# Loads of u and of unit 2's k and r moved ahead of weight strips, the flag computed inside the chain of powers, and a new order list

## The chip, the cores and the metric

The kernel runs on one core of one Trainium2 chip. The metric is the device time of one execution in microseconds (us). Before the change four runs took 508.73, 508.48, 507.45 and 509.68 us; their median is 508.6 us. Lower is better.

## What is computed

Two stages, all in float32 (the weights arrive as 64-bit words and are converted on the chip). First a linear attention with decay, for 4 batches and 8 heads of width 48 over 768 time steps, and then a feed-forward block without a non-linearity on its output:

```
cur     = einsum('bhd,bhe->bhde', u[None] * kt, vt)
y[t]    = einsum('bhd,bhde->bhe', rt, state + cur)
state   = w[None,:,:,None] * state + einsum('bhd,bhe->bhde', kt, vt)
...
x = y.transpose(0, 2, 1, 3).reshape(3072, 384)
out = (((x @ w1) * (x @ w2)) @ w3) @ w_out      # 384 -> 1024 -> 1024 -> 384
```

## The kernel before

**Units and chunks.** Time is cut into 6 chunks of 128 steps; a chunk of one batch is a unit, so there are 24 units, numbered chunk * 4 + batch. A unit's k and r (192 KB each) land in one of three `krin` buffers, its v in one of three `vnat` buffers. The decay is handled with powers of w: k and r of a unit are multiplied by the table `pn_in` (`scale`, L410) into `krs`, after which the attention inside a chunk is plain matrix products.

**Weights.** w1 and w2 come as eight strips of 768 KB (strip 0 is the first part of w1, strip 1 the first part of w2, and so on), followed by w_out and w3 in smaller pieces. They go through three `raws` buffers (`fetch`, L225) and are converted in five steps: `magnitude` on ScalarE (L360), `sign` and `high` on VectorE (L365, L368), `low` on ScalarE (L372), `total` on VectorE (L375).

**The opening** (L237 to L293) is written out by hand: the first loads on SyncE's queue; 14 dummy matmuls (`keep_busy`, L256; each shows as two in the profile); a chain of small VectorE operations (L266 to L285) that forms the powers of w in `both`; a flag that tells whether all of w lies in the range that the fast way can handle (L271, a one-row matmul L273, L287, L288); four plus four transposes of the powers (L292) and two copies into `pn_in` (L293). Every engine then reads the flag and branches (L295, L957) into one of two versions of the program. With the given data it is the fast one, and only that one runs.

**The list.** Behind the branch the order of the work on TensorE, VectorE, ScalarE and SyncE's queue is the string `ORDER` at the top of the file. Each word names a step and its indices; the kernel issues the steps in exactly that order, so each engine's order is the list with the other engines' words left out. Engines run in order; they wait for each other only where data or a buffer require it. The words that matter here (n is the unit, i the strip):

| word | step, engine | word | step, engine |
|---|---|---|---|
| kr.n, v.n, W.i | loads of k and r, of v, of a strip; SyncE's queue | U.n | `adds` (L523), TensorE: state increments, needs `krs` and `vnat` |
| d.n, e.n, f.n | `rk` (k times r, L419), `rku` (times u, L422), `dots` (sum, L426); VectorE | T.n, R.n | transposes of k and of r (L457), TensorE |
| k.n | `scale` (L410), VectorE | t.n, r.n | their copies out of PSUM (L464, L467), ScalarE |
| N.i, H.i, Q.i | `sign`, `high`, `total`; VectorE | A.n | `products` (L530), TensorE |
| M.i, L.i | `magnitude`, `low`; ScalarE | m.n | `mask` (L558), VectorE |
| g.n or h.n | `place`: the diagonal, eight ScalarE operations (L437) or one on VectorE (L431) | S.n, V.n | the unit's output in PSUM (L630, L644), TensorE |
| i.n, j.n | `state` (L541, L546, L547), VectorE | Y.n | `take`, its copy to `xT` (L652), ScalarE |
| o.n, p.n | `spread` (L555), ScalarE | a, b, c, u | x @ w1 and x @ w2 (L670), the copy (L676) and their product (L681) |
| s, B | sums for the seven-product scheme of the last matrix product (L714, L717, L701), VectorE | P, E, D | its products (L727, TensorE), their additions (L742 to L756), its stores |

The output of a unit has one PSUM tile (`psY`), so S.1 must wait until Y.0 has copied unit 0 away. The products a, b and P share two PSUM tiles (`psF`); each is free again when ScalarE or VectorE has taken it. A dot product tile `ruk` and the diagonal are needed only in g.n or h.n, the scaled k and r in all of the unit's TensorE work.

**SyncE's queue** issues the loads one after the other. An issue can itself take long, and everything behind it on the queue waits. Up to the branch the queue holds, in this order: k and r of unit 0, strip 0, v of unit 0, u (broadcast to 128 rows, L244), k and r of unit 1, strip 1, v of unit 1; then the branch, and from the list k and r of unit 2, v of unit 2, strip 2.

Of the kernel before, what the change touches and what calls it, by code (L numbers as in the profile page):

```python
# [22 lines left out]
kr.2 v.2 d.0 W.2 N.0 e.0 f.0 M.0 k.0 g.0 H.0 U.0 kr.3 T.0 d.1 R.0 k.1 L.0 e.1 kr.4 t.0 i.0 f.1 r.0 T.1 W.3 Q.0 p.0 A.0  # L23
M.1 h.1 S.0 R.1 j.0 t.1 d.2 r.1 k.2 m.0 R.2 kr.5 T.2 e.2 r.2 U.1 N.1 f.2 A.1 M.2 H.1 V.0 t.2 i.1 L.1 m.1 v.3 d.3 p.1
W.4 Q.1 Y.0 j.1 g.2 S.1 N.2 A.2 k.3 V.1 H.2 R.3 kr.6 M.3 U.2 m.2 v.4 Y.1 T.3 N.3 L.2 a.0.0.0 k.4 r.3 W.5 i.2 t.3
a.0.1.0 H.3 p.2 e.3 c.0.0.0 R.4 Q.2 L.3 S.2 j.2 b.0.0.0 M.4 W.6 f.3 Q.3 o.4 U.3 c.0.1.0 h.3 V.2 r.4 i.3 T.4 d.4 p.3
v.5 k.5 A.3 kr.7 Y.2 b.0.1.0 e.4 t.4 x.5 M.5 S.3 m.3 y.5 j.3 o.5 V.3 u.0.0.0 U.4 u.0.1.0 Y.3 v.6 A.4 f.4 M.6 k.6
a.0.0.1 g.4 N.5 N.6 b.0.0.1 H.5 c.0.0.1 m.4 L.5 a.0.1.1 z.5 H.6 u.0.0.1 L.6 x.6 W.8 b.0.1.1 c.0.1.1 W.9 i.4 y.6
a.0.2.2 Q.6 p.4 l.5 u.0.1.1 d.5 Q.5 kr.8 M.8 a.0.3.2 j.4 c.0.2.2 N.4 M.9 e.5 H.4 S.4 f.5 c.0.3.2 N.8 L.4 z.6 U.5 d.6
V.4 h.5 o.6 i.5 A.5 Y.4 kr.9 e.6 b.0.2.2 p.5 m.5 W.7 Q.4 v.7 l.6 j.5 b.0.3.2 N.9 u.0.2.2 k.7 f.6 x.7 g.6 U.6 A.6 d.7  # L30
y.7 S.5 k.8 kr.10 M.7 V.5 m.6 o.7 a.0.4.2 e.7 v.8 u.0.3.2 Y.5 f.7 z.7 x.8 b.0.4.2 d.8 c.0.4.2 y.8 h.7 kr.11 e.8 i.6
f.8 p.6 a.0.5.2 H.8 l.7 u.0.4.2 L.8 d.9 W.11 j.6 e.9 b.0.5.2 c.0.5.2 H.9 f.9 L.9 Q.8 W.12 d.10 N.7 A.7 u.0.5.2 U.7 H.7
a.0.6.2 i.7 L.7 k.9 p.7 W.10 Q.9 kr.12 a.0.7.2 j.7 c.0.6.2 x.9 Q.7 y.9 S.6 m.7 M.10 c.0.7.2 e.10 z.8 V.6 o.8 N.10 N.11
b.0.6.2 H.10 Y.6 g.8 v.9 S.7 M.11 f.10 l.8 u.0.6.2 z.9 V.7 o.9 d.11 b.0.7.2 H.11 L.10 e.11 Y.7 v.10 L.11 Q.10 W.13 g.9
Q.11 W.14 N.12 a.1.0.2 u.0.7.2 M.12 f.11 H.12 d.12 L.12 a.1.1.2 N.13 M.13 W.15 e.12 c.1.0.2 Q.12 H.13 M.14 N.14 L.13
H.14 b.1.0.2 W.16 Q.13 c.1.1.2 L.14 N.15 M.15 Q.14 W.17 H.15 b.1.1.2 L.15 u.1.0.2 W.18 Q.15 M.16 N.16 H.16 A.8 u.1.1.2
L.16 a.1.2.2 N.17 M.17 W.19 m.8 l.9 Q.16 M.18 H.17 N.18 b.1.2.2 L.17 H.18 c.1.2.2 W.20 Q.17 L.18 N.19 M.19 W.21 Q.18
G.0.0 u.1.2.2 G.0.1 K.0.0 U.8 H.19 a.1.3.2 K.0.1 i.8 L.19 k.10 p.8 W.22 N.20 M.20 kr.13 x.10 M.21 F.0 H.20 c.1.3.2
y.10 j.8 L.20 Q.19 W.23 Q.20 M.22 N.21 N.22 H.21 H.22 L.21 b.1.3.2 L.22 Q.21 W.24 X.0 Q.22 W.25 M.23 N.23 A.9 u.1.3.2
U.9 H.23 S.8 i.9 L.23 z.10 V.8 k.11 o.10 a.1.4.2 g.10 N.24 x.11 v.11 kr.14 Q.23 Y.8 m.9 y.11 b.1.4.2 p.9 W.26 N.25  # L40
f.12 c.1.4.2 j.9 l.10 d.13 e.13 S.9 u.1.4.2 o.11 A.10 z.11 a.1.5.2 m.10 a.1.6.2 c.1.5.2 l.11 a.1.7.2 c.1.6.2 b.1.5.2
V.9 u.1.5.2 U.10 c.1.7.2 v.12 G.1.0 i.10 Y.9 G.1.1 g.11 k.12 b.1.6.2 x.12 kr.15 p.10 f.13 y.12 K.1.0 d.14 b.1.7.2 M.24
j.10 M.25 e.14 u.1.6.2 K.1.1 H.24 S.10 H.25 L.24 z.12 A.11 u.1.7.2 o.12 U.11 Q.24 L.25 V.10 m.11 W.28 G.2.0 k.13 g.12
W.27 G.2.1 v.13 F.1 i.11 kr.16 Q.25 p.11 f.14 N.26 Y.10 j.11 l.12 d.15 K.2.0 x.13 K.2.1 e.15 y.13 N.27 G.3.0 X.1 U.12
S.11 k.14 o.13 V.11 i.12 kr.17 A.12 Y.11 x.14 G.3.1 v.14 g.13 a.2.0.2 z.13 m.12 K.3.0 f.15 y.14 p.12 d.16 G.4.0 K.3.1
e.16 b.2.0.2 j.12 K.4.0 c.2.0.2 l.13 U.13 u.2.0.2 S.12 k.15 z.14 o.14 V.12 i.13 A.13 Y.12 x.15 G.4.1 g.14 v.15 F.2
m.13 y.15 kr.18 K.4.1 f.16 l.14 d.17 M.26 e.17 M.27 H.26 p.13 H.27 L.26 j.13 S.13 L.27 W.29 Q.26 M.28 W.30 V.13 Q.27
o.15 z.15 N.28 A.14 Y.13 H.28 U.14 X.2 m.14 G.5.0 L.28 v.16 G.5.1 i.14 g.15 F.3 W.31 Q.28 N.29 k.16 M.29 f.17 kr.19
p.14 H.29 j.14 L.29 x.16 l.15 Q.29 S.14 y.16 K.5.0 N.30 d.18 X.3 F.4 K.5.1 N.31 e.18 o.16 z.16 G.6.0 X.4 G.6.1 K.6.0
F.5 M.30 K.6.1 H.30 M.31 L.30 H.31 Q.30 L.31 s.1.2.0 Q.31 s.1.2.1 F.6 s.1.0.0 X.5 s.1.2.3 s.1.1.0 s.1.3.0 s.1.1.2  # L50
s.1.3.1 s.1.1.1 s.1.3.3 s.1.3.2 s.1.0.1 s.1.0.2 s.1.0.3 s.1.2.2 G.7.0 X.6 s.1.1.3 U.15 K.7.0 G.7.1 i.15 P.0.0.0 K.7.1
k.17 p.15 F.7 x.17 kr.20 j.15 y.17 A.15 X.7 s.0.1.0 V.14 s.0.0.0 E.0.0.0 l.16 B.0 P.0.1.0 Y.14 v.17 s.0.0.1 g.16 m.15
a.2.1.2 s.0.0.3 B.1 E.0.1.0 f.18 B.2 a.2.2.2 c.2.1.2 B.3 s.0.1.2 s.0.0.2 s.0.2.0 b.2.1.2 d.19 c.2.2.2 s.0.2.2 s.0.2.1
s.0.1.1 s.0.2.3 s.0.3.0 b.2.2.2 s.0.1.3 s.0.3.1 u.2.1.2 s.0.3.3 e.19 s.0.3.2 P.0.0.2 wa.0 u.2.2.2 A.16 wa.1 P.0.1.2
E.0.0.2 m.16 wa.3 P.0.0.3 E.0.1.2 wb.0 P.0.0.4 wb.1 E.0.0.3 P.0.1.3 E.0.0.4 P.0.0.5 E.0.1.3 P.0.1.5 E.0.0.6 E.0.0.5
D.0.0.0 P.0.1.4 E.0.1.6 U.16 E.0.1.4 S.15 E.0.1.5 k.18 D.0.1.0 o.17 V.15 z.17 i.16 P.0.1.1 g.17 x.18 kr.21 P.0.1.6
E.0.1.1 y.18 Y.15 f.19 v.18 p.16 P.0.0.1 d.20 l.17 E.0.1.7 j.16 D.0.1.1 P.0.0.6 e.20 E.0.0.1 A.17 E.0.0.7 U.17 D.0.0.1
m.17 P.1.1.2 k.19 P.1.1.0 i.17 kr.22 x.19 p.17 S.16 E.1.1.0 j.17 y.19 z.18 o.18 V.16 E.1.1.2 U.18 g.18 P.1.0.0 k.20
v.19 i.18 kr.23 a.2.3.2 E.1.0.0 x.20 p.18 f.20 l.18 y.20 j.18 d.21 P.1.0.1 c.2.3.2 e.21 P.1.0.2 E.1.0.1 P.1.0.3
E.1.0.2 P.1.1.3 E.1.0.3 P.1.0.4 E.1.1.3 A.18 E.1.0.4 P.1.0.5 m.18 U.19 E.1.0.5 P.1.0.6 E.1.0.6 D.1.0.0 k.21 b.2.3.2  # L60
x.21 E.1.0.7 D.1.0.1 P.1.1.4 u.2.3.2 P.2.0.0 E.1.1.4 P.1.1.1 E.2.0.0 P.1.1.5 E.1.1.1 P.1.1.6 E.1.1.5 E.1.1.6 D.1.1.0
P.2.1.0 E.1.1.7 D.1.1.1 a.2.4.2 E.2.1.0 b.2.4.2 c.2.4.2 a.2.5.2 u.2.4.2 s.2.0.0 s.2.0.1 s.2.0.2 s.2.0.3 b.2.5.2
c.2.5.2 a.2.6.2 u.2.5.2 s.2.1.0 s.2.1.1 s.2.1.2 s.2.1.3 a.2.7.2 c.2.6.2 b.2.6.2 c.2.7.2 b.2.7.2 u.2.6.2 s.2.2.0
s.2.2.2 s.2.2.1 s.2.2.3 a.3.0.2 Y.16 u.2.7.2 s.2.3.0 s.2.3.2 s.2.3.1 s.2.3.3 b.3.0.2 c.3.0.2 P.2.0.2 u.3.0.2 P.2.0.1
E.2.0.2 a.3.1.2 E.2.0.1 b.3.1.2 c.3.1.2 P.2.1.2 u.3.1.2 P.2.0.3 E.2.1.2 P.2.0.4 E.2.0.3 P.2.0.5 E.2.0.4 P.2.0.6
E.2.0.6 E.2.0.5 D.2.0.0 P.2.1.1 E.2.0.7 D.2.0.1 P.2.1.3 S.17 E.2.1.3 E.2.1.1 z.19 o.19 V.17 P.2.1.4 i.19 g.19 v.20
P.2.1.5 E.2.1.4 p.19 f.21 P.2.1.6 y.21 l.19 d.22 j.19 Y.17 A.19 e.22 E.2.1.5 S.18 m.19 D.2.1.0 z.20 o.20 V.18 E.2.1.6
E.2.1.7 U.20 a.3.2.2 g.20 i.20 v.21 k.22 D.2.1.1 Y.18 f.22 p.20 x.22 S.19 l.20 z.21 V.19 d.23 c.3.2.2 e.23 o.21 A.20
b.3.2.2 g.21 m.20 y.22 v.22 Y.19 f.23 l.21 a.3.3.2 u.3.2.2 b.3.3.2 c.3.3.2 U.21 u.3.3.2 A.21 k.23 S.20 z.22 o.22
P.3.0.0 i.21 x.23 p.21 P.3.1.0 m.21 E.3.0.0 y.23 a.3.4.2 E.3.1.0 l.22 b.3.4.2 c.3.4.2 a.3.5.2 u.3.4.2 s.3.0.0 s.3.0.2  # L70
s.3.0.1 s.3.0.3 a.3.6.2 c.3.5.2 a.3.7.2 c.3.6.2 b.3.5.2 wa.2 V.20 u.3.5.2 A.22 c.3.7.2 s.3.1.0 v.23 U.22 s.3.1.2 g.22
b.3.6.2 s.3.1.1 i.22 s.3.1.3 p.22 m.22 b.3.7.2 u.3.6.2 s.3.2.0 wb.3 s.3.2.2 s.3.2.1 pa.0.0 Y.20 u.3.7.2 U.23 wb.2 S.21
s.3.3.0 ga.0.0 z.23 V.21 s.3.2.3 o.23 s.3.3.1 P.3.0.1 s.3.3.2 g.23 s.3.3.3 i.23 P.3.0.2 E.3.0.1 p.23 P.3.0.3 l.23
E.3.0.2 Y.21 A.23 E.3.0.3 S.22 m.23 V.22 P.3.1.2 Y.22 P.3.0.5 E.3.1.2 P.3.0.4 E.3.0.6 S.23 E.3.0.4 E.3.0.5 V.23
D.3.0.0 P.3.0.6 Y.23 xs.0 P.3.1.3 E.3.0.7 xs.1 D.3.0.1 P.3.1.4 xs.2 E.3.1.3 xs.3 pa.0.1 E.3.1.4 pa.0.2 ga.0.1 pa.0.3
ga.0.2 P.3.1.5 ga.0.3 P.3.1.1 E.3.1.6 E.3.1.5 D.3.1.0 P.3.1.6 E.3.1.1 pa.0.4 E.3.1.7 D.3.1.1 pa.0.5 ga.0.4 pa.0.6
ga.0.5 pa.0.7 ga.0.6 pb.0.0 ga.0.7 pb.0.1 gb.0.0 pb.0.2 gb.0.1 pb.0.3 gb.0.2 pb.0.4 mu.0.0 gb.0.3 pb.0.5 gb.0.4 pb.0.6
gb.0.5 pb.0.7 mu.0.1 gb.0.6 s.4.0.0 pa.1.0 mu.0.2 s.4.0.1 pa.1.1 ga.1.0 gb.0.7 pa.1.2 s.4.0.2 mu.0.3 ga.1.1 pa.1.3
s.4.0.3 ga.1.2 pa.1.4 ga.1.3 pa.1.5 s.5.0.0 ga.1.4 s.5.0.1 s.5.0.2 pa.1.6 s.5.0.3 ga.1.5 pa.1.7 ga.1.6 pb.1.0 ga.1.7
pb.1.1 gb.1.0 pb.1.2 gb.1.1 pb.1.3 gb.1.2 pb.1.4 mu.1.0 gb.1.3 pb.1.5 gb.1.4 pb.1.6 gb.1.5 pb.1.7 mu.1.1 gb.1.6  # L80
s.4.1.0 pa.2.0 mu.1.2 s.4.1.1 pa.2.1 ga.2.0 gb.1.7 pa.2.2 s.4.1.2 ga.2.1 mu.1.3 pa.2.3 s.4.1.3 s.5.1.0 pa.2.4 ga.2.2
s.5.1.1 pa.2.5 s.5.1.2 ga.2.4 s.5.1.3 ga.2.3 pa.2.6 ga.2.5 pa.2.7 ga.2.6 pb.2.0 ga.2.7 pb.2.1 gb.2.0 pb.2.2 gb.2.1
# [13 lines left out]
def kernel(  # L96
# [140 lines left out]
    with tc.manual_schedule(engines={PE, ACT, DVE, SP}), tc.tile_pool(name="psW", bufs=2, space=PSUM) as psW:  # L237
        nc.vector.memset(wucol, 1.0)
        for i, queue in enumerate((nc.sync, nc.scalar)):
# [3 lines left out]
        load(0, "v")  # L243
        nc.sync.dma_start(out=ub.rearrange("t h d -> t (h d)"),  # L244
                          in_=u.rearrange("h d -> (h d)").rearrange("(o n) -> o n", o=1).to_broadcast([P, DM]))
        load(1, "kr")
        fetch(1)
        load(1, "v")

# [741 lines left out]
```

## Time and profile before

| | |
|---|---|
| median of the four runs | 508.6 us (507.45 to 509.68) |
| the profiled execution: its own time, its span | 507.89 us, 506.1 us |
| TensorE / VectorE / ScalarE busy | 487.8 / 318.1 / 178.1 us of the span |
| mean granted TensorE clock | 0.992 |
| TensorE idle before a matmul, longest times | 4.1, 3.8 and 1.3 us, all before 26 us |

The span runs from the first to the last instruction; 1.8 us of the execution's own time lie outside it. The profile is one execution. A busy TensorE is not TensorE at its best: matmuls overlap, and at half the granted clock they take longer and still count as busy. In the timeline each row gives the start, the busy time, the engine, the line, the operation and, in brackets, how long the engine sat idle before it and what ended that. A row of SPq is the issue of a load; its duration is that of the issue, and the landing comes later.

### The profile page before, as it was taken

To read this page: it belongs to the slowest core of one execution; us is meant where nothing else is said; L and a number is where in the kernel's file an instruction comes from. 1 tells how busy PE (TensorE), PEld (TensorE's weight loads), DVE (VectorE), ACT (ScalarE), POOL (GpSimd) and SP (SyncE) were. 2 spreads that over 40 slices of the span, in tenths; PEclk is the share of its full clock that TensorE was granted. 3 is DMA by queue.
4 is the path that set the end of the run, shared out by engine and by line. 5 is a ranking of instruction groups with operands and counts; after the bars stand their busy time and mean duration, and the time that the engine had idled before them with its cause. 6 is when DMAs were issued, how large, how long until landed. Compare 5 with 4: busy or idle time off the path is not lost.

```text
span 506.1 us, 12288 instructions
## 1 busy us (share of the span) xinstructions
PE 487.8 (96%) x5206; PEld 322.5 (64%) x5206; DVE 318.1 (63%) x655; ACT 178.1 (35%) x448; POOL 6.0 (1%) x23
## 2 busy tenths in 40 slices
PE   5698999999999999999999999999999999999996
PEld 5576555455466666769877457855588544446996
DVE  6989987888376876685741342543445486785342
ACT  4677544876367673402400110543240000000000
POOL 4000000000000000000000000000000000000000
PEclk9889999999999999999999999999999999999999
DMA  7998896777538691302921000441010000000001
GB/s 202 207 234 228 205 244 180 194 231 242 161 98 217 180 235 32 80 0 66 222 76 47 0 0 17 129 126 62 17 35 33 31 0 1 1 0 0 32 32 68
DMA packets 96863, 52.72 MB, mean 104 GB/s; under 512 B 77728, under 2 KB 88224, under 8 KB 96800
## 3 DMA queue, kind: packets, MB, share of 16 engines
q1 hardware_dynamic: 96592, 51.85, 38.0%
q8 instruction: 43, 0.70, 0.6%
q14 instruction: 20, 0.16, 0.1%
q10 hardware_dynamic: 208, 0.00, 0.0%
HBM read 39.65 MB, written 12.19 MB: 102 GB/s over the span
## 4 chain that ended last, share of the span: by engine, by line
PE 82%; DMA 8%; DVE 3%; ACT 3%; SPq 2%; issue 1%; ACTq 0%; DVEq 0%
PE ps_b L670 14%; PE ps_a L670 14%; PE ps_w L398 8%; PE ps_b L825 5%; PE ps_a L825 5%; PE ps_s3t L727 3%; PE ps_s2t L727 3%; PE ps_s4b L727 3%; PE ps_a12b L727 3%; PE ps_s1t L727 3%; PE ps_a22t L727 3%; DMA raw<-in_moe_w_dram 3%; PE ps_a L829 3%; PE ps_b L829 3%; PE ps_a11b L727 3%; PE ps_y L630 3%
## 5 line engine op out<-in xcount | busy, mean ns | idle before, releaser
L670 PE MATMUL ps_a<-xT,w 128*128 128x512 f32 (+1 forms) x204 | 87.6, 572 | 0.9 <-ACT xT L652 0.5
L670 PE MATMUL ps_b<-xT,w 128*128 128x512 f32 (+1 forms) x204 | 88.0, 573 | 0.3 <-DVE abt L681 0.2
L670 PEld LDWEIGHTS ps_b<-xT,w 128*128 128x128 f32 x204 | 37.8, 190 | 41.2 <-issue 35.6
L670 PEld LDWEIGHTS ps_a<-xT,w 128*128 128x128 f32 x204 | 37.7, 190 | 39.2 <-issue 34.9
L681 DVE TENSOR_TENSOR abt<-ps_b,a 128x512 f32<-128x512 f32 (+1 forms) x34 | 22.2, 657 | 50.4 <-PE ps_b L670 50.2
L555 ACT COPY wide<-st 64x192 f32<-64x192 f32 x88 | 30.5, 347 | 45.5 <-PE ps_y L630 35.7
L398 PE MATMUL ps_w<-wo,w3T 128*128 128x384 f32 x128 | 42.5, 487 | 0.0
L437 ACT ACTIVATE AT<-same,dg 128x64 f32<-128x64 f32 x160 | 40.4, 336 | 5.0 <-PE ps_y L644 3.1
L676 ACT COPY a<-ps_a 128x512 f32<-128x512 f32 (+1 forms) x34 | 18.9, 556 | 46.5 <-PE ps_a L670 37.3
L398 PEld LDWEIGHTS ps_w<-wo,w3T 128*128 128x128 f32 x128 | 23.9, 190 | 15.6 <-issue 0.5
L850 DVE TENSOR_TENSOR abt<-ps_b,abt 128x512 f32<-128x512 f32 x28 | 18.9, 687 | 12.8 <-PE ps_b L829 8.4
L372 ACT ACTIVATE t<-raw 128x512 uint32<-128x512 uint32 (+2 forms) x32 | 22.6, 713 | 10.9 <-DVE w3n L368 4.9
L410 DVE TENSOR_TENSOR krs<-krin,pn_in 128x768 f32<-128x768 f32 x24 | 22.8, 951 | 1.0 <-PE ps_a L523 0.9
L630 PE MATMUL ps_y<-tt,wide 128*32 128x64 f32 x1056 | 19.7, 221 | 3.8 <-ACT xT L652 3.8
L644 PE MATMUL ps_y<-AT,vnat 64*64 64x64 f32 x1152 | 22.6, 225 | 0.6 <-DVE AT L558 0.6
L630 PEld LDWEIGHTS ps_y<-tt,wide 128*32 128x32 f32 x1056 | 15.9, 110 | 11.3 <-issue 6.6
L479 DVE STREAM_TRANSPOSE tr<-krs 128x768 f32<-128x768 f32 x19 | 18.5, 974 | 6.2 <-DMA scratch<-tr 6.1
L558 DVE COPY_PREDICATED AT<-later,ps_a 128x512 f32<-128x512 int32 x24 | 17.4, 724 | 7.8 <-PE ps_a L530 3.7
L644 PEld LDWEIGHTS ps_y<-AT,vnat 64*64 64x64 f32 x1152 | 19.6, 138 | 3.7 <-issue 1.5
L742 ACT COPY m<-ps_a11b 128x192 f32<-128x192 f32 x12 | 3.8, 315 | 49.5 <-PE ps_a11b L727 49.5
L523 PE MATMUL ps_a<-vnat,krs 64*64 64x48 f32 x704 | 16.4, 224 | 4.1 <-DVE krs L410 4.1
L523 PEld LDWEIGHTS ps_a<-vnat,krs 64*64 64x64 f32 x704 | 14.0, 138 | 9.2 <-issue 8.2
(144 smaller groups left out, 760.0 us busy)
## 6 DMA issues: line engine op xcount, KB each, us to landing
raw<-in_moe_w_dram SPq DMA_DIRECT2D x16, 512.0 KB, 5.0
scratch<-tr SPq DMA_DIRECT2D x19, 384.0 KB, 3.8
raw<-in_moe_w_dram SPq DMA_DIRECT2D x8, 768.0 KB, 6.5
tt<-scratch SPq DMA_DIRECT2D x38, 128.0 KB, 2.8
krin<-in_k_dram SPq DMA_DIRECT2D x24, 192.0 KB, 4.4
krin<-in_r_dram SPq DMA_DIRECT2D x24, 192.0 KB, 4.7
vnat<-in_v_dram SPq DMA_DIRECT2D x24, 192.0 KB, 4.0
raw<-in_moe_w_out_dram SPq DMA_DIRECT2D x8, 384.0 KB, 3.7
```

The lines of the kernel that those rows point to most:

```text
L372: nc.scalar.activation(out=part["t", i], in_=words(i)[0], func=COPY, scale=2.0 ** -29)
L398: nc.tensor.matmul(ps, lhsT=w3T[j][:, kc, :], rhs=wo[kc], start=(kc == 0), stop=(kc == KF - 1))
L410: nc.vector.tensor_mul(krs[n % NS][:, which, :, :D], kr[:, which], pn[:, which, :, :D])
L437: nc.scalar.activation(out=AT[n][:, i, p, :], in_=same, func=COPY, scale=dg[n][:, h:h + 1])
L523: nc.tensor.matmul(added(n)[rows(i), a, p, :], lhsT=kk[rows(a), 2 * p + i, :], rhs=vnat[n % NV][rows(a), 2 * p + i, 0:D], start=True, stop ...
L555: nc.scalar.copy(out=wide[a][n % 2][rows(i), :, i * D:(i + 1) * D], in_=st[units[n][1]][rows(i)])
L630: nc.tensor.matmul(yt[n][g * Q:(g + 1) * Q, a, q, :], lhsT=wide[a][n % 2][:, p, j * Q:(j + 1) * Q], rhs=rw[:, p, 2 * a:2 * a + 2] if fast ...
L644: nc.tensor.matmul(yt[n][rows(g), a, q, :], lhsT=vv[rows(a), x:x + PAD], rhs=AT[n][rows(a), h % 2, h // 2, :], start=(a, g) not in seen, s ...
L670: nc.tensor.matmul(ps, lhsT=(w1 if x == "a" else w2)[:, z, q, js], rhs=xT[c][:, q, ts], start=(q == 0), stop=(q == KM - 1))
L727: nc.tensor.matmul(ps, lhsT=of[:, m * C:(m + 1) * C], rhs=w34[:, KH * (x == 1) + j, :DH] if x < 2 else made[b][:, j, :], start=(j == 0), s ...
L825: nc.tensor.matmul(ps, lhsT=of_w, rhs=of_x, start=True, stop=x not in (2, 5, 7))
L829: nc.tensor.matmul(ps, lhsT=column(w, j, 2, half), rhs=xT[last[c]][:, 2, :], start=False, stop=True, skip_group_check=x == 6)
```

## The change

In the opening:

- SyncE's queue gets u ahead of strip 0 (it was behind strip 0 and v of unit 0), and k and r of unit 2 ahead of strip 1, so ahead of the branch; the list's first word kr.2 is gone.
- Of the 14 dummy matmuls 6 stay in front of the flag's matmul and 8 follow it.
- The two operations that finish the flag move from the end of the chain of powers to its middle.
- d.0 (k times r of unit 0) moves ahead of the branch, at the end of the opening's VectorE work. It writes into `w34`, which nothing else uses until much later, and the step d.0 of the list does nothing any more.

```
         load(0, "kr")
+        nc.sync.dma_start(out=ub..., in_=u...to_broadcast([P, DM]))
         fetch(0)
         load(0, "v")
-        nc.sync.dma_start(out=ub..., in_=u...to_broadcast([P, DM]))
         load(1, "kr")
+        load(2, "kr")
         fetch(1)
         load(1, "v")
...
-        keep_busy(14)
+        keep_busy(6)
...
                 nc.tensor.matmul(ps_out, lhsT=outs[:, NP:NP + 1], rhs=outs[:, 0:NP], start=True, stop=True)
+                keep_busy(8)
         nc.vector.reciprocal(...)
         nc.vector.tensor_copy(out=wn_in[:, 0:LEVELS, 2 * NP:, :], ...)
         nc.vector.tensor_copy(out=both[:, 1, :, HT:HT + 1], ...)
+        nc.vector.tensor_reduce(outs[0:1, NP + 1:], ps_out, AX.X, ALU.add)
+        nc.vector.tensor_scalar(flag, outs[0:1, NP + 1:], 0.0, None, ALU.is_equal)
         for l in range(LEVELS):
...
         nc.scalar.copy(out=both[:, 1, :, T:], in_=both[:, 1, :, :T])
-        nc.vector.tensor_reduce(outs[0:1, NP + 1:], ps_out, AX.X, ALU.add)
-        nc.vector.tensor_scalar(flag, outs[0:1, NP + 1:], 0.0, None, ALU.is_equal)
+        ruk0 = w34[:, 0, :].rearrange("t (h d) -> t h d", d=D)
+        nc.vector.tensor_mul(ruk0, krin[0][:, 0], krin[0][:, 1])
```

In the list the words are the same ones but for kr.2; their order differs in two parts: the first third, and the words around chunk 4 (from s.0.1.0 on), with small swaps up to the end. The first words, before and after:

```
-kr.2 v.2 d.0 W.2 N.0 e.0 f.0 M.0 k.0 g.0 H.0 U.0 kr.3 T.0 d.1 R.0 k.1 L.0 e.1 kr.4 t.0 i.0 f.1 r.0 T.1 W.3 Q.0 p.0 A.0
+v.2 d.0 W.2 e.0 f.0 M.0 k.0 N.0 g.0 H.0 U.0 kr.3 d.1 T.0 k.1 L.0 R.0 e.1 kr.4 t.0 i.0 f.1 r.0 T.1 W.3 Q.0 p.0 A.0 h.1
...
```

Taken engine by engine, the differences of the first part are these. VectorE: N.0 goes behind k.0; Q.2 goes from behind e.3 to behind f.4. ScalarE: M.1 goes from ahead of t.1 to behind r.1; t.2 goes behind Y.0; Y.1 goes ahead of M.3. TensorE: T.2 goes behind A.1; U.3 and S.3 come a little earlier. SyncE's queue: strip 4 goes ahead of v of unit 3, k and r of unit 7 ahead of v of unit 5. Around chunk 4 VectorE gets all 16 of the sums s.0 ahead of u.2.1.2 where 14 were, with e.19 and m.16 ahead of it too; the sums wa and wb go some 40 VectorE words later; TensorE's attention steps of units 16 and 17 come earlier between the products P.0 and P.1.

## The prediction

> **What bounds the kernel now.** I read the page first, then TensorE's waits, then the timeline and the table of windows for the opening. The page says that TensorE is nearly always busy:
>
> ```profile
> span 506.1 us, 12288 instructions
> ...
> PE 487.8 (96%) x5206; PEld 322.5 (64%) x5206; DVE 318.1 (63%) x655; ACT 178.1 (35%) x448; POOL 6.0 (1%) x23
> ```
>
> The span is 506.1 us, so 18.3 us are not covered. TensorE's waits, longest first:
>
> ```profile
> PE ps_a L523 <- DVE krs L410: 4.1, 1, 4.1
> PE ps_y L630 <- ACT xT L652: 3.8, 1, 3.8
> PE ps_rT L457 <- DVE krs L410: 1.3, 1, 1.3
> ```
>
> These three are 9.2 us and all lie before 26 us. The same view of 48 us to the end holds only 2.1 us in five waits (the longest 0.6). So from 48 us on the list can lose time but hardly gain any, and a gain has to come from the opening. The rows that set the first and the second wait:
>
> ```profile
> 3.84 1.74 SPq L244 DMA_DIRECT2D ub<-in_u_dram  x1
> ...
> 7.43 0.14 DVE L288 TENSOR_SCALAR flag<-outs 1x1 int32<-1x1 f32 x1
> ...
> 8.43 0.56 DVE L419 TENSOR_TENSOR ruk<-krin 128x384 f32<-128x384 f32 x1 [0.85 <-DVE flag L288]
> ...
> 10.16 0.56 DVE L422 TENSOR_TENSOR ruk<-ruk,ub 128x384 f32<-128x384 f32 x1 [0.71 <-DMA ub<-in_u_dram]
> ...
> 11.23 0.95 DVE L410 TENSOR_TENSOR krs<-krin,pn_in 128x768 f32<-128x768 f32 x1
> 11.29 3.77 SPq L206 DMA_DIRECT2D krin<-in_r_dram  x1
> ...
> 15.97 0.67 SPq L225 DMA_DIRECT2D raw<-in_moe_w_dram  x1
> ...
> 22.53 0.89 ACT L360 ACTIVATE w<-raw 128x768 f32<-128x768 f32 x1 [1.91 <-DMA raw<-in_moe_w_dram]
> ...
> 25.32 0.48 ACT L652 COPY xT<-ps_y 128x384 f32<-128x384 f32 x1
> ```
>
> The reader should see two chains. In the first, VectorE waits 0.85 us for the branch and 0.71 us for u, and does k.0 last; TensorE's first real matmul (U.0) starts at 12.43, 0.25 us behind k.0's end at 12.18. In the second, strip 2 is issued at 15.97 and lands at 22.5 (the chain of waits gives 6.53 us); M.2 on ScalarE waits for it, and behind M.2 stand t.2, L.1, p.1 and Y.0, without which S.1 cannot start (25.94).
>
> **Why strip 2 comes so late.** Each time three 192 KB loads follow a strip, the third one's issue lasts until the strip has landed. Unit 2's r: 11.29 + 3.77 = 15.06, strip 1 landing at 8.44 + 6.8 = 15.2. Unit 4's k: 19.14 + 3.10 = 22.24, strip 2 landing at 22.5. Unit 1's r: 6.10 + 2.30 = 8.40, strip 0 landing at 2.51 + 6.0 = 8.5. Strip 2 stands behind such a held load.
>
> **The change, part by part.**
>
> Flag. Before, its matmul ran at 7.02, behind 14 dummies (28 rows, 5.94 us from 1.15, so 0.21 us each). Now 6 end at about 3.7, the flag's input is ready at 3.92, and the matmul ends near 4.1. The two flag operations (7.25 to 7.57) go into the chain of powers and push its end from 7.14 to 7.44. The 8 other dummies take 16 x 0.21 = 3.4 us and end at 7.5, so the transposes start at 7.55 where they started at 7.25; pn_in is ready at 9.3 where it was 9.02. Cost: 0.3 us on pn_in, hidden until k.0.
>
> d.0 ahead of the branch. It runs from 7.44 to 8.0; its k and r were issued at 1.41 and 1.89 and landed by 6.1 (3.0 and 4.2 us), and they stand ahead of u still. If they were late, the branch would be late with them. VectorE then reads the flag. Before, that showed as 0.85 us. On ScalarE, whose last copy was still running when the flag was there, it cost 0.06 us (copies until 9.02, M.0 at 9.08). So e.0 starts between 8.05 and 8.85; I take 8.05, since d.0 is such a cover.
>
> u. It lands at 10.07 before (3.84 + 6.23). Ahead of strip 0 and v it is issued at 2.5 and has 384 KB ahead of it instead of 1344 KB. r, with 192 KB ahead, took 4.2 us; with 4.2 to 6.2 u lands at 6.7 to 8.7. Of the 0.71 us at most 0.65 is left (8.7 against 8.05).
>
> k.0. e.0 0.5 and f.0 0.5 (start to start in the rows), so 9.1; k.0 then waits for pn_in at 9.3 and ends at 10.25. U.0 starts at 10.5, with the branch uncovered at 11.1. Before: 12.43. It also needs v of unit 0, which landed at 9.4 and now stands behind u: one load of that size lands 0.7 us after another, or 1.8 us later if u's issue keeps its 1.74 us; so 10.1 to 11.2. **Gain at U.0: 1.2 to 1.9 us.** N.0 (0.5) now comes behind k.0, so VectorE is ahead by 1.3 from d.1 on (11.6 instead of 12.96). Unit 1's k and r landed at 10.8 and 11.3; they are not moved but by u's issue, 1.8 at the most.
>
> ScalarE: M.0 at 9.3, g.0 at 10.2 (11.41 before, where it waited 1.43 for f.0), L.0, t.0 at 13.1 (14.14). M.1 goes behind r.1, so t.1 no longer waits 0.9 for it, and strip 1, later by two loads, has until about 16.8. It was at 15.2 and comes at about 17: nothing or 0.2 us.
>
> VectorE's m.0, which frees TensorE for U.1, ends at 18.6 to 18.9 (19.81).
>
> k and r of unit 2 ahead of strip 1. The loads behind strip 1 are now v of unit 1, v of unit 2 and strip 2: two loads and no third, so no issue is held there. Counting: unit 1's r is held until strip 0 lands as before, at 8.5 to 10.2; then k and r of unit 2, strip 1, v of unit 1, each when an earlier load has landed, 0.7 us apart: 12.5; the branch on this queue 0.7 (9.71 + 0.49 to 10.88 before); v of unit 2; strip 2 at 14.3, where it was 15.97. With the same 6.5 us it lands at 20.8. **1.7 us earlier.** The bytes ahead of it are the same, so it cannot gain more than the queue's idle stretches: in the table of windows the loads move 163 GB/s from 13.4 to 16.7 and 261 before it.
>
> Y.0. M.2 from 20.8 to 21.7; L.1 (H.1 is done at 21.3) to 22.6; p.1 0.7, to 23.3; Y.0, with t.2 (0.56) now behind it, to 23.8. **S.1 at 23.9 instead of 25.94: 2.0 us.** Q.1 follows L.1 at 22.6 (24.72): 2.1 us.
>
> After that VectorE is the one that paces TensorE: it is 9.35 of 10 us busy from 30 to 50. Both it and TensorE are ahead by about 2, and Y.1 ahead of M.3 takes a 1.23 us wait for strip 3 off the path of S.2. Loads of strips 5 and 6 must come earlier too; strip 4 ahead of v of unit 3 takes one held issue (25.72, 3.12 us) from ahead of it. I count nothing more: the sum is 2.0.
>
> The rest of the list. No instruction is added or removed, so the 2.1 us of waits from 48 us on become 0 at best. The place that I checked by hand is u.2.1.2. VectorE was ready for it 0.70 us before its matmul. With two more sums (0.34 each), e.19 (0.5) and m.16 (0.7), which waits for A.16, it ends at 223.6 on the old clock; P.0.1.2 wants the tile at 224.5. That is 0.9 us of room. I take 0, bounds -2 and +4.
>
> **The clock.** The table of windows shows half clock twice, each after a stretch in which TensorE was busy 0.97 or 1.06 us of 3.4; after 1.97 it stayed full:
>
> ```profile
> 10.00:13.40 3.40, 0.97 (x35) 0.94 (x36) 3.20 (x5) 1.99 (x9) 0.00 (x0) 0.99 0.88 261
> 13.40:16.70 3.30, 3.26 (x43) 2.56 (x41) 3.30 (x7) 3.16 (x7) 0.00 (x0) 0.50 0.78 163
> ...
> 20.20:23.60 3.40, 1.97 (x114) 1.73 (x112) 2.84 (x6) 1.49 (x3) 0.00 (x0) 1.00 0.96 235
> 23.60:27.00 3.40, 1.06 (x62) 1.00 (x66) 2.81 (x6) 3.33 (x10) 0.00 (x0) 1.00 0.99 212
> 27.10:30.40 3.30, 3.30 (x87) 2.76 (x79) 1.45 (x2) 2.07 (x7) 0.00 (x0) 0.50 1.09 263
> ```
>
> With idle stretches of 1.9 us the changed kernel may stay above that point. Worth in the second stretch, where TensorE has no idle behind it: R.3 1.11 us against 0.63 elsewhere, U.2 1.10 against 0.68, V.1 1.45 against 0.88, so up to 1.5 us. I keep it as the lower end. The Trainium skill (TensorE: Matmul & The Clock Gate, "What's actually happening") says that the clock falls after at least one idle window of about 3.4 us. Here it fell after windows with some 30% of work, so the row decides; by the page's rule the gaps of before would have cost nothing, and this term would be 0.
>
> **Rivals.**
>
> (1) The loads keep the pace. If u's issue takes its 1.74 us wherever it stands, strip 0 and all behind it come up to 1.8 later, strip 2 lands at 22 or so, and S.1 at 25.1 to 25.4: gain 0.6, 508.0 us. For it: loads are 80 to 100% busy from 2 to 48 us. Against it: u's issue stood behind three loads in flight, and may have been held by them.
>
> (2) Slower: VectorE falls behind TensorE around chunk 4, and the wait for a P tile that u.2.1.2 has room for comes at many of the 28 products P.0 to P.1. The nearest rows are the waits of 0.6 and 0.4 us at 254 and 256 for the same tiles. Eight such at 0.45 cost 3.6 us; from five on (2.25) they outweigh the gain. 508.6 - 2.0 + 3.6 = 510.2 us. Against it: VectorE is only 70% busy from 200 to 250.
>
> (3) Both half-clock stretches go: 2.0 + 1.5, 505.1 us.
>
> (4) The change doesn't do what it says: the waits of M.2 and U.0 go, and the next in-order engine (VectorE with k.2, H.1, Q.1) waits as long in their place. The gain is 0 to 1 us, 507.6 to 508.6; I count it with (1).
>
> **How the numbers follow.** Against the profiled execution: 507.89 - 2.0 = 505.9 (span 504.1). It lies 0.7 below the median of 508.6, so by the median the forecast is 506.6 us. Chances: forecast (gain 1.5 to 3) 0.46; rival 3 0.14; rivals 1 and 4 0.27; rival 2 0.13. A difference under 0.3% (1.5 us) is about what a measurement of this kernel cannot tell from none. So faster 0.60, same 0.27, slower 0.13. The range reaches from 1.2 below rival 3, for waits saved later, to 0.8 short of rival 2's price: 503.9 to 509.4.
>
> **What would show it.** Right: U.0 at 10.5 to 11.1; no wait for u; strip 2 issued near 14.3 and landed near 20.8; S.1 near 23.9; no more than 2.5 us of TensorE waits behind 48 us. Wrong: a u issue still 1.7 us long with strip 0 at 10; strip 2 at 22; waits for P tiles between 210 and 260 us.

## The result, and the profile after

| | before | after |
|---|---|---|
| median of the compared runs | 508.7 us (78 runs) | 507.65 us (52 runs) |
| ratio, 95% interval | | 0.9981 [0.9972, 0.999] |
| profiled execution: own time, span | 507.89, 506.1 us | 507.55, 505.8 us |

The change makes the kernel about 1.0 us faster, half of the 2.0 us forecast. The page of the kernel after hardly differs:

```profile
span 505.8 us, 12285 instructions
...
PE 488.1 (97%) x5206; PEld 322.9 (64%) x5206; DVE 318.0 (63%) x655; ACT 178.0 (35%) x448; POOL 6.0 (1%) x23
```

TensorE's waits in the kernel after, largest total first (total us, times, longest):

```profile
PE ps_a L531 <- DMA vnat<-in_v_dram: 4.2, 2, 3.4
PE ps_y L638 <- ACT xT L660: 3.3, 1, 3.3
PE ps_a L538 <- ACT kT L504: 1.4, 2, 0.9
```

The first wait, once for k.0, is now for v of unit 0 (3.4 of the 4.2 us); the second is still that of S.1 for Y.0. The timeline of the kernel after (start, busy, engine, line, operation, idle before it and what ended that):

```profile
2.51 0.74 SPq L242 DMA_DIRECT2D ub<-in_u_dram  x1
...
5.13 5.72 SPq L206 DMA_DIRECT2D krin<-in_r_dram  x1
...
7.13 0.55 DVE L293 TENSOR_TENSOR w<-krin 128x384 f32<-128x384 f32 x1
...
9.14 0.56 DVE L430 TENSOR_TENSOR w<-w,ub 128x384 f32<-128x384 f32 x1 [1.46 <-DMA ub<-in_u_dram]
...
11.08 0.90 ACT L365 ACTIVATE w<-raw 128x768 f32<-128x768 f32 x1 [1.97 <-DMA raw<-in_moe_w_dram]
...
11.81 0.68 PE L531 MATMUL ps_a<-vnat,krs 64*64 64x48 f32 x32 [3.38 <-DMA vnat<-in_v_dram]
...
15.44 2.66 SPq L225 DMA_DIRECT2D raw<-in_moe_w_dram  x1
...
23.37 0.89 ACT L365 ACTIVATE w<-raw 128x768 f32<-128x768 f32 x1 [2.09 <-DMA raw<-in_moe_w_dram]
...
25.66 0.48 ACT L660 COPY xT<-ps_y 128x384 f32<-128x384 f32 x1
```

The issue of u takes 0.74 us where it took 1.74, and yet VectorE waits 1.46 us for it: u lands at 9.02, 3.27 us behind r of unit 0 (5.75 in the trace). All loads behind it are late: strip 0 lands at 10.99 (before: 8.55), the issue of unit 1's r is held 5.72 us (2.30), and U.0 starts at 11.81, only 0.6 earlier than before. Strip 2 is issued 0.5 us earlier and lands 0.85 us later (23.35 against 22.50); S.1 starts at 26.28 instead of 25.94. So in this profile nothing has been gained by S.1.

The table of windows (length; busy us of TensorE, its weight loads, VectorE, ScalarE and GpSimd, with instructions; granted clock, DMA share, GB/s) shows what u's load does. Before:

```profile
4.00:6.00 2.00, 2.00 (x11) 2.00 (x10) 1.82 (x15) 0.00 (x0) 2.00 (x8) 1.00 0.91 223
6.00:8.00 2.00, 1.93 (x17) 1.73 (x16) 1.40 (x9) 0.46 (x2) 0.92 (x2) 1.00 1.08 350
```

After:

```profile
4.00:6.00 2.00, 2.00 (x12) 1.96 (x12) 1.81 (x16) 0.00 (x0) 2.00 (x7) 1.00 0.66 142
6.00:8.00 2.00, 1.62 (x15) 1.46 (x15) 1.65 (x9) 0.41 (x1) 0.92 (x2) 1.00 0.82 203
```

From 4 to 6 and from 6 to 8 us the loads move 142 and 203 GB/s where they moved 223 and 350, though the next load's issue is held from 5.13 us on.

### The profile page after: what moved, and what is told of

Its sections match the earlier page's. It is cut to its first block, busy times and chain, and to the rows that moved or that the text cites. A ratio compares the mean times of both kernels' runs of the same rounds, so it can differ in the third digit from the quotient of the medians.

```text
span 505.8 us, 12285 instructions
## 1 busy us (share of the span) xinstructions
PE 488.1 (97%) x5206; PEld 322.9 (64%) x5206; DVE 318.0 (63%) x655; ACT 178.0 (35%) x448; POOL 6.0 (1%) x23
## 4 chain that ended last, share of the span: by engine, by line
PE 83%; DMA 10%; ACT 2%; DVE 2%; SPq 2%; issue 1%; ACTq 0%; DVEq 0%
PE ps_a L678 15%; PE ps_b L678 14%; PE ps_w L403 7%; PE ps_b L833 5%; PE ps_a L833 5%; DMA raw<-in_moe_w_dram 4%; PE ps_a11b L735 3%; PE ps_s2t L735 3%; PE ps_a12b L735 3%; PE ps_s4b L735 3%; PE ps_s1t L735 3%; PE ps_y L638 3%; PE ps_y L652 3%; PE ps_s3t L735 3%; PE ps_a L538 3%; PE ps_b L837 3%
## 5 line engine op out<-in xcount | busy, mean ns | idle before, releaser
L689 DVE TENSOR_TENSOR abt<-ps_b,a 128x512 f32<-128x512 f32 (+1 forms) x34 | 22.3, 657 | 44.9 <-PE ps_b L678 44.8
L403 PEld LDWEIGHTS ps_w<-wo,w3T 128*128 128x128 f32 x128 | 23.9, 190 | 15.7 <-issue 0.5
L638 PEld LDWEIGHTS ps_y<-tt,wide 128*32 128x32 f32 x1056 | 16.4, 112 | 10.1 <-issue 6.1
L538 PEld LDWEIGHTS ps_a<-tt,kT 64*64 64x64 f32 x768 | 15.0, 141 | 9.5 <-ACT kT L504 2.5
L504 ACT COPY kT<-tt 128x512 f32<-128x512 f32 x19 | 11.7, 617 | 24.1 <-DMA tt<-scratch 20.9
```

Of the source, the lines that this page charges most:

```text
L403: nc.tensor.matmul(ps, lhsT=w3T[j][:, kc, :], rhs=wo[kc], start=(kc == 0), stop=(kc == KF - 1))
L538: nc.tensor.matmul(upper(n)[rows(a), i, p, :], lhsT=kT[n][rows(i), p, rows(a)], rhs=rT[n][rows(i), p, 2 * a:2 * a + 2], start=True, stop=True)
L638: nc.tensor.matmul(yt[n][g * Q:(g + 1) * Q, a, q, :], lhsT=wide[a][n % 2][:, p, j * Q:(j + 1) * Q], rhs=rw[:, p, 2 * a:2 * a + 2] if fast ...
L689: nc.vector.tensor_mul(abt[c, j][:, parts_of_tokens[part]], factor["b", c, j, part], factor["sa", c, j, part])
```

## Experiments

Every ratio is to runs of the kernel before on the same chip, with its 95% interval. Two questions: did the opening bring the gain, as forecast, or the list; and why does u's load cost so much?

**Opening and list apart.** First the changed opening with the list of before (its first word kr.2 left out, as those loads are already made):

```
 (after) ORDER = list of before without "kr.2"
```

> The changed kernel's opening with the list of before (without its first word kr.2, which the opening now issues). Theory (the opening as it stands brings nothing by S.1, and the gain of some 1 us comes from the new list between 27 and 90 us): 508.3 to 509, so no gain over the kernel before. Rival (the opening is what gains, the list only shuffles waits): 507.2 to 507.8, as the changed kernel.

Measured: 510.33 us, 1.003 [1.0008, 1.0053]. The opening as built costs 1.5 us. Then the reverse:

```
 (before) ORDER = "kr.2" + list of after
```

> The opening of before with the changed kernel's list (its first word kr.2 put back, d.0 done behind the branch). Theory (the list alone gains): Y.0 ahead of t.2 and Y.1 ahead of M.3 take S.1 to 25.4 and leave S.2 without the wait for strip 3; 507.0 to 507.8, as good as the changed kernel or better. Rival (the opening gains): 508.3 to 509, as the kernel before.

Measured: 506.1 us, 0.9948 [0.9928, 0.9969]. The list alone gains 2.65 us; the two ratios multiply to 0.998, that of the whole change. TensorE's waits in this kernel:

```profile
PE ps_a L523 <- DVE krs L410: 3.7, 1, 3.7
PE ps_a L523 <- DMA vnat<-in_v_dram: 1.6, 1, 1.6
PE ps_y L630 <- ACT xT L652: 1.4, 1, 1.4
```

The wait of S.1 for Y.0 is 1.4 us where it was 3.8 (S.1 starts at 24.46), with the old order of loads up to the branch. That is one execution, though: the kernel with only the first part of this list (next) begins with the same instructions, and in its profile S.1 starts at 27.08. So the gain is shown by the runs' times, and its place is not shown by the profiles. A wait for a v load has come in its place, since the list puts strip 4 ahead of v of unit 3.

**Which part of the list.** The new list up to s.0.1.0, then the old one, and the reverse:

```
 (before) ORDER = "kr.2" + words of after up to s.0.1.0 + words of before from there on
 (before) ORDER = words of before up to s.0.1.0 + words of after from there on
```

> The opening of before; of the new list the words up to s.0.1.0, and from there on the old list. Theory (the list gains in its first third, where ScalarE's order changes): 0.994 to 0.996 of the kernel before, as the whole new list gave (0.9948). Rival (the part made anew around chunk 4 gains too): 0.997 to 0.999, and the rest of the 0.5% comes from the second part.

> The kernel before, with the new list only from s.0.1.0 on (the part around chunk 4 and behind). Theory (TensorE is full there, and the waits of 2.1 us can at best become 0): 0.997 to 1.000. Rival (the second part holds half of what the whole new list gave): 0.9965 to 0.9980, with the first part's 0.9970 the whole 0.9948.

Measured: first part 506.09 us, 0.997 [0.9951, 0.9989]; second part 508.05 us, 0.9984 [0.9964, 1.0004]. The first part gains; the second is worth little or nothing. Three moves of the first part that the prediction had named:

```
-M.1 h.1 ... t.1 d.2 r.1 k.2 ... V.0 t.2 i.1 ... Y.0 j.1 ... M.3 U.2 m.2 v.4 Y.1 T.3
+h.1 ... t.1 d.2 r.1 M.1 k.2 ... V.0 i.1 ... Y.0 t.2 j.1 ... Y.1 U.2 m.2 M.3 v.4 T.3
```

> The kernel before with three moves on ScalarE and nothing else: M.1 from ahead of t.1 to behind r.1, t.2 behind Y.0, Y.1 ahead of M.3. Theory (these three are the list's gain: TensorE no longer waits at S.1 and S.2 behind conversions that wait for strips): 0.995 to 0.997 of the kernel before; S.1 0.6 earlier. Rival (the gain is spread over the many small moves): 0.999 to 1.000.

Measured: 509.23 us, 1.002 [0.9998, 1.0042]. These moves alone bring nothing, so the gain lies in other words of the first part (or in these only together with others). There are many: the first part reaches to word 675 of 1326, and compared engine by engine some 40 of its words change place, where the list under "The change" names only the ten nearest the start. Which of them gain was not tried further.

**Where the opening loses.** u's load back behind strip 0 and v of unit 0, all else as changed:

```
-        (u's load)
         fetch(0)
         load(0, "v")
+        (u's load)
```

> The changed kernel with the load of u put back behind v of unit 0, where it was before the change; all else as changed. Theory (u ahead of strip 0 leaves the loads idle from 5 to 8 us, because its 128 reads of one row come slowly, and holds strip 0, v and r): strip 0 lands at 8.6 instead of 10.99, unit 1's r is issued by 8.5 instead of 10.85, strip 2 lands near 21 instead of 23.35; e.0 waits for u until 10.1, so k.0 ends near 12.0 and U.0 starts near 12.2; S.1 near 24.5 instead of 26.28; the time is 0.5 to 1.5 us under the changed kernel, 506 to 507. Rival (the loads' total sets strip 2's landing whatever the order): strip 2 lands at 22.5 to 23.5 as before, S.1 at 26, and the time is that of the changed kernel or up to 0.5 above it.

Measured: 506.17 us, 0.9939 [0.9917, 0.9961]: 0.4% faster than the kernel after. The same move alone in the kernel before, the other way round:

> The kernel before with one move: the load of u ahead of strip 0. Theory (u alone, right behind k and r of unit 0, costs the loads some 2 us, and the loads set the pace until strip 6 has landed): u lands near 9, strip 0 near 11, strip 6 near 45.5, and the time is 1.5 to 2.5 us over the kernel before, 1.003 to 1.005. Rival (the cost needs the rest of the new opening too): within 0.1% of the kernel before.

Measured: 511.02 us, 1.0047 [1.0024, 1.007]. Strip 0 lands at 10.87, u at 8.81, as in the kernel after. This is more than the spread of single profiles: in the three kernels with u in front strip 0 lands at 10.87 to 11.09, in the nine with u behind strip 0 and v at 7.87 to 9.95. Both sides give the same price, 2.1 to 2.4 us, for u in front. Then everything on SyncE's queue back in its old order (u behind v of unit 0, kr.2 behind the branch), with flag, dummies, d.0 and the new list kept:

> The changed kernel with all loads in the order of before (u behind v of unit 0, k and r of unit 2 behind the branch); the flag inside the chain of powers, the split dummies, d.0 ahead of the branch and the new list stay. Theory (k and r of unit 2 ahead of strip 1 bring little, since the loads as a whole set strip 2's landing; flag and d.0 bring little too): 0.993 to 0.996 of the kernel before, as with u alone put back (0.9939) and as with the old opening and the new list (0.9948). Rival (k and r ahead of the branch are worth the 1.7 us that I gave them): 0.997 to 0.998.

Measured: 505.9 us, 0.9964 [0.994, 0.9987]. Its interval overlaps that of u moved back alone; whether unit 2's k and r stand ahead of strip 1 or behind the branch makes no difference that these runs can tell.

**Why u is slow.** 128 partitions read the one row of u, 1536 bytes, 128 times. In the next kernel the load has the same place, packets and bytes, but 128 different rows (of r, so that y comes out different):

```
-    in_=u.rearrange("h d -> (h d)").rearrange("(o n) -> o n", o=1).to_broadcast([P, DM]))
+    in_=r.rearrange("b h s d -> (b h s d)").rearrange("(o n) -> o n", n=DM)[0:P])
```

> The changed kernel, but u's load reads 128 different rows of 1536 bytes (the first ones of r) in place of one row 128 times; the diagonal of the attention is computed with these values in place of u. The load stands at the same place and moves the same bytes. Theory (128 reads of one row are slow): the load lands at 6.7 to 7.0 instead of 9.02, strip 0 at 9.0 to 9.3 instead of 10.99, U.0 at 10.5, strip 2 near 21.5; the time is 1 us or more under the changed kernel. Rival (the first large packets behind the first small ones are slow, whatever they read): the load lands near 9 and strip 0 near 11, as in the changed kernel, and the time is the same within 0.5 us.

Measured: 505.48 us, 0.9941 [0.9916, 0.9966]. The load lands at 6.50 instead of 9.02, strip 0 at 8.61 instead of 10.99. The load in the kernel after and in this one (the last number is us from issue to landing):

```profile
ub<-in_u_dram SPq DMA_DIRECT2D x1, 192.0 KB, 6.5
ub<-in_r_dram SPq DMA_DIRECT2D x1, 192.0 KB, 4.0
```

Timeline of this kernel:

```profile
2.51 0.79 SPq L242 DMA_DIRECT2D ub<-in_r_dram  x1
...
5.00 3.37 SPq L206 DMA_DIRECT2D krin<-in_r_dram  x1
...
10.37 0.68 PE L531 MATMUL ps_a<-vnat,krs 64*64 64x48 f32 x32 [1.92 <-DVE krs L415]
...
12.69 3.67 SPq L225 DMA_DIRECT2D raw<-in_moe_w_dram  x1
```

and its windows:

```profile
4.00:6.00 2.00, 2.00 (x19) 1.95 (x18) 1.81 (x16) 0.00 (x0) 2.00 (x8) 1.00 1.03 255
6.00:8.00 2.00, 0.81 (x8) 0.66 (x7) 1.79 (x10) 0.40 (x1) 0.94 (x3) 1.00 1.07 357
```

255 and 357 GB/s against 142 and 203: in this place it is the source of the load that slows the queue. It takes both, the source and the place, since the same load behind strip 0 and v costs nothing that shows. U.0 starts at 10.37 and no longer waits for v.

**Is an earlier U.0 worth anything?** u moved back, and k.0 and M.0 ahead of e.0 and f.0, which need u:

```
-v.2 d.0 W.2 e.0 f.0 M.0 k.0 N.0 g.0
+v.2 d.0 W.2 M.0 k.0 e.0 f.0 N.0 g.0
```

> The changed kernel with u back behind v of unit 0, and in the list k.0 ahead of e.0 and f.0, so that the wait for u (10 us) no longer stands ahead of U.0. U.0 starts at 9.7 to 10.3 where it was 12.2 with u put back alone. Theory (an earlier U.0 brings nothing, because strip 2's landing near 21 sets S.1): within 0.2% of u put back alone, 0.992 to 0.996 of the kernel before. Rival (the opening's computing is what ends last): 1.5 us less, 0.990 to 0.991.

Measured: 505.02 us, 0.9945 [0.9921, 0.9969], with U.0 at 10.42 instead of 12.23. Beside 0.9939 that is no gain that these runs can tell for 1.8 us; the 1.5 us of the rival (0.990 to 0.991) lie outside the interval. In the profiles 1.0 us of the 1.8 comes back at TensorE's next wait (1.86 us against 0.88), the half clock lasts 13.65 us instead of 10.24, and S.1 starts at 25.58 against 25.32.

**Do the loads set the pace?** The kernel before with k and r read as 128 contiguous rows of 1536 bytes in place of 1024 pieces of 192 bytes (other values, so that y comes out different):

```
-                nc.sync.dma_start(out=dst, in_=src[b, :, ts, :].rearrange("h t d -> t h d"))
+                (k, r) nc.sync.dma_start(out=dst..., in_=src...[n * C * DM:(n + 1) * C * DM].rearrange("(t e) -> t e", e=DM))
```

> The kernel before, but k and r of each unit are read as 128 rows of 1536 bytes that lie one behind the other, in place of 1024 pieces of 192 bytes; the attention then works on other values than the reference's. Every load stands where it was and moves the same bytes, and no other engine's work changes. Theory (the loads set the pace of the opening): strip 6 lands 3 us or more ahead of its 43.4, and the end follows it, 2 to 5 us less, 0.990 to 0.996. Rival (VectorE and ScalarE set it, the loads only look full): strip 6 comes earlier but the time stays within 0.5 us, 0.999 to 1.001.

Measured: 503.79 us, 0.9907 [0.9871, 0.9942]; strip 6 lands at 37.53 instead of 43.41. The issue of unit 1's r is not held any more in this kernel's timeline (before: 2.30):

```profile
5.92 0.57 SPq L211 DMA_DIRECT2D krin<-in_r_dram  x1
```

So earlier loads do shorten the kernel. Set the landing of strip 6 against the end of the last matmul, in the profiles of all kernels but the one under "A better version", whose trace has no landing for strip 6:

| kernel | strip 6 lands | last matmul ends | difference |
|---|---|---|---|
| new opening, old list | 47.2 | 505.64 | 458.4 |
| before, u ahead | 45.4 | 506.72 | 461.4 |
| old opening, first part | 44.9 | 502.08 | 457.2 |
| before, three moves | 44.3 | 502.25 | 458.0 |
| after | 44.2 | 501.76 | 457.6 |
| before | 43.4 | 501.93 | 458.5 |
| old opening, second part | 43.4 | 500.93 | 457.5 |
| old opening, new list | 43.1 | 501.39 | 458.3 |
| distinct rows | 42.7 | 499.48 | 456.8 |
| u back, k.0 first | 42.6 | 498.57 | 456.0 |
| u back | 41.9 | 499.14 | 457.2 |
| loads back | 41.2 | 497.60 | 456.4 |
| large packets | 37.5 | 497.67 | 460.2 |

In eleven of the first twelve the end follows strip 6 within 2.6 us, though strip 6 itself moves by 6. The one outside is the kernel before with u ahead, where TensorE also waits 2.1 us for `xT` at 45 us. In the last the loads are ahead: 5.9 us earlier bring 4.3. A single profile is not the median, though: three kernels with the same order of loads (old opening with the new list or its first part, and loads back) differ by up to 3.7 us at strip 6, so the table shows the tie, not the worth of one edit. The Trainium skill (DMA: Bandwidth & Descriptors, "Why small descriptors are slow (HBM only)") names about 3 cycles on top of one per 32 bytes for each packet. By that eight packets of 192 bytes would take 72 cycles and one of 1536 bytes 51, a factor of 1.41, an estimate from the page; the packets in this trace took 15 ns and 65 ns, a factor of 120/65 = 1.85. The direction agrees; the measured price of small pieces is higher.

**A better version.** u as one row of 1536 bytes, spread over the partitions by a matmul with ones (in place of two of the eight dummies) and copied by ScalarE:

```
-        nc.sync.dma_start(out=ub..., in_=u...to_broadcast([P, DM]))
+        nc.sync.dma_start(out=urow, in_=u...)
...
-                keep_busy(8)
+                keep_busy(6)
+                nc.tensor.matmul(ps_u, lhsT=busy[0:1], rhs=urow, start=True, stop=True)
+                nc.scalar.copy(out=ub.rearrange("t h d -> t (h d)"), in_=ps_u)
```

> The changed kernel, but u is loaded once, as one row of 1536 bytes at the place of the 128-row load, and spread to 128 rows by a matmul with ones (in place of two of the dummy matmuls) and a copy on ScalarE, which is idle there. Theory (the 128 reads of one row were the cost, and loads set the pace): strip 0 lands at 8.0 to 8.6, strip 6 1 us ahead of the kernel with u put back (41.9); U.0 at 10.4; the time is at or under that kernel's, 0.990 to 0.994. Rival (an extra 0.5 us on TensorE and ScalarE ahead of the powers' transposes delays pn_in and with it everything): 0.995 to 0.998.

Measured: 505.22 us, 0.9932 [0.9907, 0.9958], faster than the kernels before and after; from u simply put back (0.9939) it can't be told apart. Strip 0 lands at 8.53, strip 2 at 20.33, and S.1 starts at 23.54. Some of its windows, cut where the granted clock changes:

```profile
6.41:9.83 3.42, 2.49 (x14) 1.34 (x12) 2.34 (x7) 1.85 (x4) 0.51 (x2) 1.00 1.08 272
9.83:13.24 3.41, 2.19 (x38) 2.13 (x39) 3.30 (x5) 3.33 (x10) 0.00 (x0) 0.50 0.96 190
...
20.06:23.48 3.42, 1.77 (x75) 1.40 (x67) 3.00 (x6) 2.98 (x6) 0.00 (x0) 1.00 0.99 192
23.48:26.90 3.42, 2.67 (x116) 2.27 (x120) 3.39 (x6) 2.91 (x10) 0.00 (x0) 1.00 0.90 265
```

The half clock of the opening is still there; the second stretch, around 27 us in the kernels before and after, is gone in this profile.

## Why the prediction was half right

The sign came out right by luck. The sum had 2.0 us from the opening and 0 from the list; by the runs the opening costs 1.5 us and the list gains 2.65. The pieces, from the ratios above (each known to some 0.002): the list 0.9948; u in front 0.9981 / 0.9939 = 1.0042; the rest of the opening (flag, d.0, order of unit 2's loads) 0.9939 / 0.9948 = 0.9991, not to be told from 1. Their product is 0.9981.

**Flag and pn_in: right.** The flag operations stand at 5.15 to 5.48, and the copies of pn_in end at 9.10 (forecast 9.3).

**d.0: right.** It runs at 7.13 to 7.68 (forecast 7.44 to 8.0). The 0.85 us for the branch no longer shows, but VectorE then waits 1.46 us for u, so the cover brought nothing here. With distinct rows, where the load is there in time, e.0 starts 0.17 us behind d.0.

**u: the step that failed.** "With 4.2 to 6.2 u lands at 6.7 to 8.7" took the load for one like any other, whose price is its place. It landed at 9.02, and the same load from distinct rows at 6.50. The prediction's worry was the issue of 1.74 us; that one was indeed held by the queue (0.74 now). In its old place, behind strip 0 and v, no single packet of it took more than 107 ns in the kernel before and 455 ns in seven others; in front, in three kernels, the slowest took 1218 to 1442 ns.

**U.0: "Gain at U.0: 1.2 to 1.9 us" failed twice.** It was 0.6, because v of unit 0 landed at 11.67 (forecast 10.1 to 11.2). And it would have been worth little: U.0 at 10.42 gave no gain over 12.23 that the runs can tell.

**"Two loads and no third, so no issue is held there" failed.** Strip 2 is then itself the third load behind strip 1 (so a held load need not be one of 192 KB; and counting u, the held r of unit 1 was the fourth behind strip 0): its issue lasts from 15.44 to 18.10, until strip 1 has landed (18.27). With distinct rows it is 12.69 to 16.37 and 16.54. Hence "it lands at 20.8. 1.7 us earlier" became 23.35. Without the slow u it was 21.63 (distinct rows) and 20.33 (u by matmul), both with that issue held. "S.1 at 23.9 instead of 25.94: 2.0 us" became 26.28, and 24.61 and 23.54 in these two. A difference of 1 us here means little: the kernel with the old opening and the new second part begins as the kernel before does, and its strip 2 lands at 21.61 and its S.1 starts at 25.06 (22.50 and 25.94 before). Nor does S.1 pass into the time one to one, as the sum took it: 23.54, 24.46 and 25.58 came with medians of 505.22, 506.1 and 505.02 us.

**"The rest of the list. I take 0" failed.** I had looked for its worth only behind 48 us, where the second part indeed brings little (0.9984 [0.9964, 1.0004]), and priced the first part by three ScalarE moves that bring nothing. The first part gains 0.3%.

**Rivals.** (1), the loads keep the pace, is what happened, though through slow packets and not through a long issue; its 508.0 us is closer than the forecast's 506.6, by chance too, as it put S.1 at 25.1 to 25.4 and had nothing from the list. (2) did not happen: the waits of TensorE for P tiles at 254 and 256 us (0.63 and 0.45) are gone, and the two new waits between 210 and 260 us (0.49 and 0.15) are not for a P tile. (3) did not happen. In the windows of the kernel after, cut where the clock changes, it falls to half after windows with 0.85 and 0.11 us of work, and the first time it stays there twice as long as before:

```profile
9.25:12.66 3.41, 0.85 (x34) 0.83 (x35) 2.99 (x5) 1.58 (x5) 0.00 (x0) 1.00 0.87 201
12.66:16.07 3.41, 2.38 (x12) 1.86 (x10) 3.13 (x7) 3.39 (x11) 0.00 (x0) 0.50 0.96 212
16.07:19.48 3.41, 3.16 (x62) 2.29 (x60) 3.19 (x6) 0.97 (x3) 0.00 (x0) 0.50 1.11 268
...
22.90:26.31 3.41, 0.11 (x11) 0.06 (x5) 2.20 (x4) 2.90 (x6) 0.00 (x0) 1.00 0.77 150
26.31:29.72 3.41, 3.41 (x106) 3.12 (x107) 2.57 (x4) 2.50 (x10) 0.00 (x0) 0.50 1.02 294
```

The prediction's point, between 1.06 and 1.97 us of work, holds for these and for the second stretch of the version with the matmul (1.77 us, full). It does not hold for that kernel's first stretch, where the clock fell after a window with 2.49 us: the busy time of one window doesn't settle it.

What a stretch is worth can be estimated from the clocks of the single executions. Over some 265 executions of these kernels, each against the mean of its own kernel, 0.001 more of mean granted clock goes with 0.15 us less time (standard error 0.025). A stretch of 3.41 us at half clock takes 0.0034 off the mean of a 506 us span, so it goes with about 0.5 us, where the prediction allowed up to 1.5. By the same measure a part of u's price may be clock: the runs after have a mean of 0.987, those with u back and with distinct rows 0.992, which would be about 0.7 of the 2.1 us. This goes together in the runs; it isn't shown to be the cause.

**Open.** Which words of the list's first part gain; why 128 reads of one row are slow in that place; how much of their price comes by way of the clock; and what in a window makes the clock fall.

## What to carry to other kernels

Before a load is moved forward, ask what it reads: a small tensor that is broadcast to all partitions by a load can hold up everything behind it when it stands among the first loads. Here one row spread by a matmul with ones (0.9932) and the load left behind strip 0 and v (0.9939) both avoided that. Where the loads set the pace, the number to forecast is the landing of the last one that the work waits for, not the start of the first matmul. Split a change into its parts before judging it: here a gain of 0.5% hid a loss of 0.4%. And take the worth of an edit from the runs' times: two executions with the same beginning differed by 2.6 us at S.1.

## What the runs showed of the hardware

- 128 reads of one row of 1536 bytes, right behind loads of 192-byte pieces, landed 6.51 us after their issue, and 3.99 us when the rows were distinct. Single packets took up to 1442 ns, and 660 ns with distinct rows, where the median is 65 ns; in eight kernels with this load behind strip 0 and v the slowest packet took 67 to 455 ns.
- An issue was held until just before a strip ahead landed, and not only for 192 KB loads: that of strip 2 (768 KB) ended at 18.10, 16.37 and 15.70 us in three kernels, where strip 1 landed at 18.27, 16.54 and 16.01.
- The granted clock changes at multiples of about 3.41 us, but it stayed full behind a window with 1.77 us of TensorE work and fell behind another with 2.49 us. Over the single executions 0.001 of mean granted clock went with 0.15 us.
